# Row-shaped score matmuls with one late transpose, and four instead of five VectorE batches, in a decode attention kernel

## The chip, the cores and the metric

The kernel runs on one core of a Trainium2 chip. The metric is device time in microseconds (us): medians over several executions, with the lowest and highest beside them where they matter. Runs of one kernel are compared with runs of the kernel before on the same chip. Where a run is set against the changed kernel ("after"), the two were taken in different calls; the kernel before was timed in each of these calls, and its medians there lie between 2827.4 and 2829.4 us.

Engine names are those of the profile: PE is TensorE, DVE is VectorE, ACT is ScalarE, POOL is GpSimd, SP is the queue that issues the transfers.

## The reference

Two independent attention blocks, A and B, do one decode step each. For 8 batches and 32 heads, a query of 128 numbers meets 4096 cached keys and values. Everything is bf16.

```python
q = (x @ wq).reshape(B, Sq, H, Dh).transpose(0, 2, 1, 3)        # B=8, Sq=1, H=32, Dh=128
scores = jnp.einsum("bhqd,bhkd->bhqk", q, k_cache) * (Dh ** -0.5)   # Sk=4096 keys
p = softmax(scores, axis=-1)
o = jnp.einsum("bhqk,bhkd->bhqd", p, v_cache)
return o.transpose(0, 2, 1, 3).reshape(B, Sq, H * Dh) @ wo
# the outputs of A and B are concatenated
```

Each key and value is used once. K and V of one batch and head are 1 MB each; there are 2 x 32 x 8 = 512 such pairs, so 1,074 MB must be read whatever the arithmetic does.

## The kernel before

The kernel walks over 64 groups (one head of one block, 8 batches each), batch by batch. The scores of a batch are made on one of two paths. `DVB` lists the batches of each group that go to VectorE; the others go to TensorE.

The VectorE path makes one fused multiply-and-add instruction for each 128 keys. The profile shows two for it (L409 of the page below: 10,240 products and 10,240 reads of an accumulator in 320 VectorE batches), so a batch costs 64 instructions.

```python
NKB = 3
DVB = list(cfg.get("DVB", (1, 2, 4, 5, 7)))          # five of eight batches on VectorE
PEB = [b for b in range(NB) if b not in DVB]          # 0, 3, 6 on TensorE
# ... (cut)
def dqk_item(n, k):                                   # quarter k of VectorE batch n
    # ... (waits cut: K landed, q replicated, previous batch done)
    for jj in range(8):
        j = 8 * k + jj
        ins = d.tensor_tensor_reduce(junk[:, j, :], Kb[:, kslot, j * 128:(j + 1) * 128], q_rep[:, par, r, :],
                                     1.0, 0.0, ALU.mult, ALU.add, S2[:, par, r, j:j + 1])
```

The TensorE path transposes K (pairs of bf16 are moved as one f32), ScalarE copies the result from PSUM to SBUF (`KT`), and small matmuls make the scores, with K as the stationary operand and a query of two columns as the moving one.

```python
def emit_T(n, q):                                     # 4 transposes, q = 0..3
    # ... (cut)
    for tt in range(4):
        t = q * 4 + tt
        ins = pe.transpose(dst[:, tt * 128:(tt + 1) * 128], kf[:, t * 128:(t + 1) * 128], ident_f[:])
def emit_QK(n, q):                                    # 8 small matmuls
    # ... (cut)
    for tt in range(4):
        t = q * 4 + tt
        # ... (cut)
        for e in range(2):
            ins = pe.matmul(S[:, c:c + 2], lhsT=ktb[:, t * 256 + e:(t + 1) * 256:2],
                            rhs=Qe[:, G % 2, pe_rank[b], e, :], start=(e == 0), stop=(e == 1))
```

All transfers are issued by SP, in one order. K has 6 buffers (`NK`), V has 8. A buffer of K is free when its transposes (TensorE batch) or its dot products (VectorE batch) are done.

```python
w = [k_released(n - NK)] if n >= NK else []
# ... (cut)
sp.dma_start(Kb[:, n % NK, :], Ks[blk][b, h].rearrange("(p j) d -> p (j d)", p=128))
```

## Time and profile before

| | before |
|---|---|
| time, median of 15 runs | 2827.81 us (2822.08 to 2833.07) |
| VectorE busy, instructions | 80%, 20,935 |
| TensorE busy, instructions (matmuls and weight loads) | 68%, 2 x 15,328 |
| K and V transfers on q1, share of 16 DMA engines | 96.2% |
| instruction fetches: q8, q14 | 124, 204 packets |

These are lines of the profile's page. The first gives the span, the second the busy time of each engine with its share and instruction count. PEclk is the granted TensorE clock and DMA the busy share of the DMA engines, both in tenths for 40 equal slices of the span. The q lines are DMA queues: packets, MB, share of 16 engines. Then come the shares of the chain of waits, and groups of instructions (count, busy us, mean ns of one, idle time before them).

```profile
span 2829.2 us, 58099 instructions
PE 1921.2 (68%) x15328; PEld 1228.2 (43%) x15328; DVE 2271.6 (80%) x20935; ACT 685.6 (24%) x1997; POOL 52.1 (2%) x138
...
PEclk7888788887888887888778888888778887788888
DMA  9999999999999999998999989999899998999996
...
q1 hardware_dynamic: 165056, 1107.43, 96.2%
q8 instruction: 124, 2.03, 0.3%
q14 instruction: 204, 1.67, 0.1%
...
DMA 52%; DVE 31%; PE 13%; SPq 2%; issue 1%; ACT 0%; DVEq 0%; POOL 0%; POOLq 0%
...
L409 DVE CUSTOM_DVE_ANT_0 junk<-Kb,q_rep 128x128 bf16<-128x128 bf16 x10240 | 2211.2, 286 | 323.9 <-DMA Kb<-in_A_k_cache_dram 146.7
L269 PE MATMUL ps<-Vb,Ppad 128*32 128x512 bf16 x4096 | 1010.3, 397 | 7.1 <-ACT Ppad L385 3.0
L229 PE MATMUL ps<-ident_f,Kb 128*128 128x128 f32 x3072 | 621.5, 386 | 508.0 <-DMA Kb<-in_B_k_cache_dram 266.5
L409 DVE DVE_READ_ACCUMULATOR2_ANT S<- 128x1 f32 x10240 | 833.5, 81 | 0.1
...
L250 PE MATMUL ps<-Qe,KT 128*128 128x2 bf16 x6144 | 182.8, 163 | 0.2
```

No compute engine is full; the DMA engines nearly are. But "96% on average" hides something. The windows view shows the busy time of each engine in stretches of 10 us, and in its last three columns the granted clock, the DMA share and GB/s:

```profile
core 0: us, PE busy (x) PEld busy (x) DVE busy (x) ACT busy (x) POOL busy (x), PEclk, DMA share, GB/s
2020.00:2030.00 10.00, 3.70 (x22) 2.83 (x21) 9.94 (x95) 0.46 (x2) 0.00 (x0) 0.76 1.01 425
2030.00:2040.00 10.00, 8.71 (x76) 5.04 (x74) 7.18 (x68) 1.92 (x4) 0.00 (x0) 0.90 0.79 306
2040.00:2050.00 10.00, 5.75 (x27) 4.39 (x28) 8.86 (x84) 3.20 (x6) 0.00 (x0) 0.66 0.15 38
2050.00:2060.00 10.00, 3.38 (x44) 1.66 (x41) 6.85 (x63) 0.00 (x0) 0.37 (x1) 0.79 1.01 416
```

Between 2040 and 2050 us the DMA engines moved 38 GB/s instead of about 420. In 5-us windows the share goes down to 0.06 or 0.07, which is one engine of 16. Such a hole comes about every 350 us, some 15 us after SP issues each load of the next projection weights.

The landing records of the trace point to the engine whose part of a transfer lands last. They do not number the engines; that it is the same one each time is read from its even pace. The records hold 16 raises of a semaphore for each of the 1,096 transfers of K, V and the weights (17,536 of 17,572 records). I read each raise as one of the 16 engines whose own part has landed. That is a reading; what speaks for it is the spacing: in this run the fourteenth raise comes within about 2 us of the first (1.5 us on average), and the sixteenth on average 14.2 us after the fourteenth (and 13.8 us after the fifteenth). So read, one engine lags by some six 64-KB shares of a transfer. My reading of a hole is that the other fifteen have no work left that the buffers allow, and the last one catches up; inside it the trace's packets follow each other singly, 0.31 us per 8 KB.

The waits of the SP queue (who waited for whom: us, times, longest) say that the next K transfer is often held until VectorE frees a buffer. That can be read in two ways: VectorE is late, or the K data was late to VectorE because its sixteenth part was.

```profile
SPq L715 <- DVE S L409: 1269.4, 296, 22.7
SPq L720 <- PE ps L269: 305.8, 174, 9.9
...
SPq L715 <- PE ps L229: 21.1, 11, 9.2
```

### The profile page before, as it was taken

The numbers are of one execution on the slowest core, as the hardware profiler recorded it, in microseconds if no ns is written. First come the engines' busy times: TensorE is split into PE (matmuls) and PEld (weight loads), VectorE is DVE, ScalarE is ACT, GpSimd is POOL, SyncE is SP. The second block draws the span as 40 slices with busy tenths as digits, with TensorE's granted clock in tenths as the row PEclk, the third lists the DMA queues.
The fourth block names the chain that finished last, engine by engine and source line by source line (L and its number), as shares of the span: only waits on it lengthen the run. The fifth ranks groups of instructions, "written<-read, shape, count | busy, mean of one in ns | idle before, by whom it ended". The sixth has DMA issues, their size and how long they took to land.

```text
span 2829.2 us, 58099 instructions
## 1 busy us (share of the span) xinstructions
PE 1921.2 (68%) x15328; PEld 1228.2 (43%) x15328; DVE 2271.6 (80%) x20935; ACT 685.6 (24%) x1997; POOL 52.1 (2%) x138
## 2 busy tenths in 40 slices
PE   4676666766667676766767667776667667666666
PEld 3444444444344444444444444444444444444443
DVE  7988788877888878888787887888878888788885
ACT  2222222222122222222222222222222222222222
POOL 0000000000000000000000000000000000000000
PEclk7888788887888887888778888888778887788888
DMA  9999999999999999998999989999899998999996
GB/s 360 420 419 416 375 414 398 389 393 370 420 406 390 378 385 420 405 397 359 404 411 400 396 353 399 419 418 401 334 420 419 410 401 342 420 408 396 398 395 251
DMA packets 165384, 1111.13 MB, mean 393 GB/s; under 512 B 17568, under 2 KB 17568, under 8 KB 33984
## 3 DMA queue, kind: packets, MB, share of 16 engines
q1 hardware_dynamic: 165056, 1107.43, 96.2%
q8 instruction: 124, 2.03, 0.3%
q14 instruction: 204, 1.67, 0.1%
HBM read 1107.33 MB, written 0.03 MB: 391 GB/s over the span
## 4 chain that ended last, share of the span: by engine, by line
DMA 52%; DVE 31%; PE 13%; SPq 2%; issue 1%; ACT 0%; DVEq 0%; POOL 0%; POOLq 0%
DVE junk L409 30%; DMA Kb<-in_B_k_cache_dram 27%; DMA Kb<-in_A_k_cache_dram 24%; PE ps L229 7%; PE ps L269 5%; DVE S L409 1%; SPq L715 1%; SPq L720 1%; DMA Vb<-in_B_v_cache_dram 1%; PE ps L332 1%; DVE Qe L453 0%; DVE acc L476 0%; DVEq L755 0%; PE ps L312 0%; SPq L737 0%
## 5 line engine op out<-in xcount | busy, mean ns | idle before, releaser
L409 DVE CUSTOM_DVE_ANT_0 junk<-Kb,q_rep 128x128 bf16<-128x128 bf16 x10240 | 2211.2, 286 | 323.9 <-DMA Kb<-in_A_k_cache_dram 146.7
L269 PE MATMUL ps<-Vb,Ppad 128*32 128x512 bf16 x4096 | 1010.3, 397 | 7.1 <-ACT Ppad L385 3.0
L229 PE MATMUL ps<-ident_f,Kb 128*128 128x128 f32 x3072 | 621.5, 386 | 508.0 <-DMA Kb<-in_B_k_cache_dram 266.5
L409 DVE DVE_READ_ACCUMULATOR2_ANT S<- 128x1 f32 x10240 | 833.5, 81 | 0.1
L229 PEld LDWEIGHTS ps<-ident_f,Kb 128*128 128x128 f32 x3072 | 555.1, 205 | 548.6 <-DMA Kb<-in_B_k_cache_dram 284.7
L366 ACT COPY KT<-ps 128x512 f32<-128x512 f32 x768 | 436.5, 589 | 1192.9 <-PE ps L229 1192.7
L269 PEld LDWEIGHTS ps<-Vb,Ppad 128*32 128x32 bf16 x4096 | 379.9, 100 | 504.8 <-issue 138.2
L312 PE MATMUL ps<-ident,q_all 128*128 128x128 bf16 x320 | 54.2, 292 | 373.3 <-DVE Qe L453 324.2
L417 ACT CAST q_rep<-ps 128x512 bf16<-128x512 f32 (+1 forms) x128 | 54.6, 427 | 782.9 <-PE ps L312 782.9
L312 PEld LDWEIGHTS ps<-ident,q_all 128*128 128x128 bf16 x320 | 28.8, 122 | 392.5 <-DVE Qe L453 328.3
L250 PEld LDWEIGHTS ps<-Qe,KT 128*128 128x128 bf16 x6144 | 167.7, 97 | 54.2 <-issue 53.5
L250 PE MATMUL ps<-Qe,KT 128*128 128x2 bf16 x6144 | 182.8, 163 | 0.2
L476 DVE TENSOR_TENSOR acc<-ps,acc 128x64 f32<-128x64 f32 x62 | 13.9, 225 | 162.0 <-PE ps L332 162.0
L385 ACT ACTIVATE Ppad<-S,negM 128x32 bf16<-128x32 f32 x320 | 100.0, 318 | 0.0
L323 PEld LDWEIGHTS ps<-Sel,Dg_sb 32*128 32x128 f32 x512 | 61.6, 186 | 28.8 <-issue 26.5
L323 PE MATMUL ps<-Sel,Dg_sb 32*128 32x8 f32 x512 | 67.2, 253 | 4.0 <-ACT q_all L417 2.8
L695 POOL PARTITION_ALL_REDUCE M_sb<-m_sb x64 | 23.5, 367 | 2486.5 <-DVE m_sb L629 2486.5
L385 ACT ACTIVATION_READ_ACCUMULATOR Ppad<-S,negM 128x1 f32 x320 | 63.4, 198 | 0.0
L586 ACT COPY Dg_sb<-ps 32x512 f32<-32x512 f32 x64 | 36.8, 575 | 105.3 <-PE ps L269 105.3
L385 ACT ACTIVATE Ppad<-ps,negM 128x32 bf16<-128x32 f32 x192 | 54.6, 284 | 19.9 <-DVE negM L652 19.5
L385 ACT ACTIVATION_READ_ACCUMULATOR Ppad<-ps,negM 128x1 f32 x192 | 38.6, 201 | 0.0
L652 DVE TENSOR_SCALAR negM<-M_sb 128x8 f32<-128x8 f32 x64 | 11.0, 172 | 31.6 <-POOL M_sb L695 31.6
(36 smaller groups left out, 199.0 us busy)
## 6 DMA issues: line engine op xcount, KB each, us to landing
Kb<-in_A_k_cache_dram SPq DMA_DIRECT2D x256, 1024.0 KB, 24.8
Vb<-in_A_v_cache_dram SPq DMA_DIRECT2D x256, 1024.0 KB, 26.7
Kb<-in_B_k_cache_dram SPq DMA_DIRECT2D x256, 1024.0 KB, 25.1
Vb<-in_B_v_cache_dram SPq DMA_DIRECT2D x256, 1024.0 KB, 26.8
wq_sb<-in_A_wq_dram SPq DMA_DIRECT2D x4, 2048.0 KB, 32.4
wo_sb<-in_A_wo_dram SPq DMA_DIRECT2D x32, 256.0 KB, 25.3
wq_sb<-in_B_wq_dram SPq DMA_DIRECT2D x4, 2048.0 KB, 33.5
wo_sb<-in_B_wo_dram SPq DMA_DIRECT2D x32, 256.0 KB, 25.5
```

The source lines that it names most:

```text
L229: ins = pe.transpose(dst[:, tt * 128:(tt + 1) * 128], kf[:, t * 128:(t + 1) * 128], ident_f[:])
L250: ins = pe.matmul(S[:, c:c + 2], lhsT=ktb[:, t * 256 + e:(t + 1) * 256:2], rhs=Qe[:, G % 2, pe_rank[b], e, :], start=(e == 0), stop=(e == 1))
L269: ins = pe.matmul(Dg(par), lhsT=Ppad[:, par, b, c].rearrange("p a m -> p (a m)"), rhs=Vb[:, vslot, c * 512:(c + 1) * 512], start=(b == 0 a ...
L312: ins = pe.matmul(Mp_f[:, r * 128:(r + 1) * 128], lhsT=q_all[:, G, b:b + 1].broadcast_to([128, 128]), rhs=ident[:], start=True, stop=True)
L323: ins = pe.matmul(Mp_f[:, 0:NB], lhsT=Dg_sb[0:32, par, jj * 128:(jj + 1) * 128], rhs=Sel[0:32, jj, :], start=(jj == 0), stop=(jj == 3))
L332: ins = pe.matmul(Mp_f[:, c * NB:(c + 1) * NB], lhsT=wo_sb[:, G % 2, c * 128:(c + 1) * 128], rhs=oT[:, G % 2, :], start=True, stop=True)
L366: return a.copy(dst, src)
L385: return a.activation(Ppad[:, par, b, :, b, :], src.rearrange("p (c m) -> p c m", m=4), ACTF.Exp, bias=negM[:, par, pos[b]:pos[b] + 1], sc ...
L409: ins = d.tensor_tensor_reduce(junk[:, j, :], Kb[:, kslot, j * 128:(j + 1) * 128], q_rep[:, par, r, :], 1.0, 0.0, ALU.mult, ALU.add, S2[:, ...
L417: return eng.copy(dst, src) if COPY_ENG == "act" else eng.tensor_copy(dst, src)
L586: return a.copy(Dg_sb[:, G % 2, :], Dg(G % 2))
L715: return sp.dma_start(Kb[:, n % NK, :], Ks[blk][b, h].rearrange("(p j) d -> p (j d)", p=128))
```

## The change

The change has two parts. One batch of each group moves from VectorE to TensorE: VectorE keeps 1, 3, 5, 7. And the scores of a TensorE batch are made the other way round: the query is the stationary operand (32 columns, mostly zeros, one row for each batch and key position) and K the moving one, 512 columns at a time. All TensorE batches of a group accumulate into one PSUM bank, as rows; ScalarE copies the bank out and TensorE transposes it once per group. As that bank is taken from the K transposes, they have two banks instead of three. The intent is to relieve VectorE, the busiest compute engine, and to pay for it with fewer TensorE instructions.

```diff
-    NKB = 3
-    DVB = list(cfg.get("DVB", (1, 2, 4, 5, 7)))
+    NKB = 2
+    DVB = list(cfg.get("DVB", (1, 3, 5, 7)))
...
-                        t = q * 4 + tt
+                        t = 4 * tt + q
                         ins = pe.transpose(dst[:, tt * 128:(tt + 1) * 128], kf[:, t * 128:(t + 1) * 128], ident_f[:])
...
-                    for tt in range(4):
-                        t = q * 4 + tt
-                        c = b * NJ + 2 * t
-                        for e in range(2):
-                            ins = pe.matmul(S[:, c:c + 2], lhsT=ktb[:, t * 256 + e:(t + 1) * 256:2],
-                                            rhs=Qe[:, G % 2, pe_rank[b], e, :], start=(e == 0), stop=(e == 1))
+                    r = pe_rank[b]
+                    for e in range(2):
+                        first = (r == 0 and q == 0 and e == 0)
+                        last = (r == NPE - 1 and q == NQ - 1 and e == 1)
+                        ins = pe.matmul(Srow, lhsT=QeP[:, G % 2, r, e, q, :],
+                                        rhs=ktb[:, q * 1024 + e:(q + 1) * 1024:2],
+                                        start=first, stop=last, skip_group_check=True)
...
+        def emit_ST(G):
...
+                for tl in range(4):
+                    ins = pe.transpose(dst[:, tl * RW:(tl + 1) * RW], Srow_sb[0:RW, tl * 128:(tl + 1) * 128], ident_f[0:RW, 0:RW])
...
+                def f(a, G=G):
+                    return a.copy(Srow_sb[0:RW, :], Srow)
+                add("act", f"SREV{G}", w, [(act_sr, 1)], f)
```

Left out: the two query permutations (QP) become two bursts with a VectorE copy after each, the exponentials and the maximum read the transposed bank, and the waits follow.

More of the change, by code (lines that the diff above doesn't have):

```diff
@@ L100, in bass_concat_heads__mha_block_cached__mha_block_cached__decode_kernel @@
         HM2 = E(nc.sbuf_tensor("HM2", [128, 2], f32))
-        Qe = E(nc.sbuf_tensor("Qe", [128, 2, max(NPE, 1), 2, 2], bf16))
+        RW = 8 * max(NPE, 1)
+        QeP = E(nc.sbuf_tensor("QeP", [128, 2, max(NPE, 1), 2, 4, RW], bf16))
+        Srow_sb = E(nc.sbuf_tensor("Srow_sb", [32, 512], f32))
         acc = E(nc.sbuf_tensor("acc", [128, NBLK, NCO * NB], f32))
@@ L117, in Slin, with Sq @@
             return ps[:, 3 + par, :]
+        Srow = ps[0:RW, 2, :]
+        def Sq(par):
+            return ps[:, 3 + par, 0:4 * RW]
         def Dg(par):
@@ L140, in bass_concat_heads__mha_block_cached__mha_block_cached__decode_kernel @@
         s_hm = sem("s_hm")
+        act_sr, pe_st = sem("act_sr"), sem("pe_st")
         def head_info(n):
@@ L191, in bass_concat_heads__mha_block_cached__mha_block_cached__decode_kernel @@
             for G in range(NG):
-                pe_extras.setdefault(slot_QR(G), []).append(("QP", G))
+                for e in range(2):
+                    pe_extras.setdefault(slot_QR(G), []).append(("QP", (G, e)))
         for G in range(NG):
@@ L245, in f @@
                     ktb = KT[:, e_idx(n) % 2, :]
-                    for tt in range(4):
-                        t = q * 4 + tt
-                        c = b * NJ + 2 * t
-                        for e in range(2):
-                            ins = pe.matmul(S[:, c:c + 2], lhsT=ktb[:, t * 256 + e:(t + 1) * 256:2],
-                                            rhs=Qe[:, G % 2, pe_rank[b], e, :], start=(e == 0), stop=(e == 1))
+                    r = pe_rank[b]
+                    for e in range(2):
+                        first = (r == 0 and q == 0 and e == 0)
[3 more added lines that the diff above has]
+                                        start=first, stop=last, skip_group_check=True)
                     return ins
@@ L297, in emit_QS, with emit_QP, f @@
             return f
-        def emit_QP(G):
+        def emit_QP(G, e):
+            def f(pe):
+                return pe.matmul(Mp_f[:, 0:NB], lhsT=Perm[:, e, :], rhs=q_all[:, G, :], start=True, stop=True)
+            return f
+        def emit_ST(G):
+            par = G % 2
             def f(pe):
                 ins = None
-                for e in range(2):
-                    ins = pe.matmul(Mp_f[:, e * NB:(e + 1) * NB], lhsT=Perm[:, e, :], rhs=q_all[:, G, :],
-                                    start=True, stop=True)
+                dst = Sq(par)
+                for tl in range(4):
+                    ins = pe.transpose(dst[:, tl * RW:(tl + 1) * RW], Srow_sb[0:RW, tl * 128:(tl + 1) * 128], ident_f[0:RW, 0:RW])
                 return ins
@@ L378, in exp_item, with f @@
                     w.append((pool_L, G - 1))
-            if b in pe_rank:
-                src = Sp(par)[:, b, :]
-            else:
-                src = S2[:, par, dv_rank[b], :]
-            def f(a, G=G, b=b, par=par, src=src):
-                return a.activation(Ppad[:, par, b, :, b, :], src.rearrange("p (c m) -> p c m", m=4),
+            if b in pe_rank and T1:
+                src = Sq(par).rearrange("p (t h u r) -> p r t h u", t=4, h=2, u=4, r=NPE)[:, pe_rank[b]]
+                dst = Ppad[:, par, b, :, b, :].rearrange("p (t h) m -> p t h m", h=2)
+            elif b in pe_rank:
+                src = Sp(par)[:, b, :].rearrange("p (c m) -> p c m", m=4)
+                dst = Ppad[:, par, b, :, b, :]
+            else:
+                src = S2[:, par, dv_rank[b], :].rearrange("p (c m) -> p c m", m=4)
+                dst = Ppad[:, par, b, :, b, :]
+            def f(a, G=G, b=b, par=par, src=src, dst=dst):
+                return a.activation(dst, src,
                                     ACTF.Exp, bias=negM[:, par, pos[b]:pos[b] + 1], scale=SCALE,
@@ L444, in burst_reads, with f @@
                 elif kind == "QP":
-                    G = idx
-                    w = [rd_burst_wait(("QP", G))]
+                    G, e = idx
+                    w = [rd_burst_wait(("QP", (G, e)))]
                     if G >= 2:
                         w.append((pe_qk, NPE * (G - 1)))
-                    def f(d, G=G):
-                        src = Mp_f[:, 0:2 * NB].rearrange("p (e b) -> p b e", e=2)
-                        src = src[:, PEB[0]:PEB[0] + pe_step * (NPE - 1) + 1:pe_step, :]
-                        return d.tensor_tensor(Qe[:, G % 2], src.unsqueeze(3).broadcast_to([128, NPE, 2, 2]),
-                                               HM2[:, :].unsqueeze(1).unsqueeze(1).broadcast_to([128, NPE, 2, 2]), ALU.mult)
-                    add(which, f"QPC{G}", w, [(dve_mp, 1)], f)
+                    def f(d, G=G, e=e):
+                        src = Mp_f[:, PEB[0]:PEB[0] + pe_step * (NPE - 1) + 1:pe_step]
+                        dst = QeP[:, G % 2, :, e, :, :].rearrange("p r c (c2 j r2) -> p r c c2 j r2", r2=NPE, c2=4, j=2)
+                        base = dst[:, 0, 0, 0, :, 0]
+                        (ps_, pn_), (js_, jn_) = base.ap
+                        r_st = dst[:, :, 0, 0, 0, 0].ap[1][0] + dst[:, 0, 0, 0, 0, :].ap[1][0]
+                        c_st = dst[:, 0, :, 0, 0, 0].ap[1][0] + dst[:, 0, 0, :, 0, 0].ap[1][0]
+                        diag = bass.AP(base.tensor, base.offset, [[ps_, pn_], [r_st, NPE], [c_st, 4], [js_, jn_]])
+                        return d.tensor_tensor(diag, src.unsqueeze(2).unsqueeze(3).broadcast_to([128, NPE, 4, 2]),
+                                               HM2[:, :].unsqueeze(1).unsqueeze(1).broadcast_to([128, NPE, 4, 2]), ALU.mult)
+                    add(which, f"QPC{G}.{e}", w, [(dve_mp, 1)], f)
                 elif kind == "OEX":
@@ L517, in bass_concat_heads__mha_block_cached__mha_block_cached__decode_kernel @@
                     if q == 0:
-                        w.append(dve_done(("QP", G)) if T1 else dve_done(("QS", G // HQ)))
-                        if pe_rank[b] == 0 and G >= 2:
+                        w.append(dve_done(("QP", (G, 1))) if T1 else dve_done(("QS", G // HQ)))
+                        if pe_rank[b] == 0 and G >= 1 and T1:
+                            w.append((act_sr, G))
+                        if pe_rank[b] == 0 and G >= 2 and not T1:
                             w.append((sm_m, NSM * (G - 1)))
@@ L523, in bass_concat_heads__mha_block_cached__mha_block_cached__decode_kernel @@
                     add("pe", f"QK{n}.{q}", w, [(pe_qk, 1)] if q == NQ - 1 else [], emit_QK(n, q))
+                if T1 and pe_rank[b] == NPE - 1:
+                    w = [(act_sr, G + 1)]
+                    if G >= 2:
+                        w.append((sm_m, NSM * (G - 1)))
+                        w.append((act_P, NB * (G - 2) + NB))
+                    add("pe", f"ST{G}", w, [(pe_st, 1)], emit_ST(G))
             if DL <= i < N + DL:
@@ L540, in bass_concat_heads__mha_block_cached__mha_block_cached__decode_kernel @@
                 elif kind == "QP":
-                    G = idx
-                    w = [dve_done(("QS", G // HQ)), (s_hm, 1)] + pe_burst_waits(("QP", G))
-                    add("pe", f"QP{G}", w, [(pe_mp, 1)], emit_QP(G))
+                    G, e = idx
+                    w = [dve_done(("QS", G // HQ)), (s_hm, 1)] + pe_burst_waits(("QP", (G, e)))
+                    add("pe", f"QP{G}.{e}", w, [(pe_mp, 1)], emit_QP(G, e))
                 elif kind == "OEX":
@@ L577, in bass_concat_heads__mha_block_cached__mha_block_cached__decode_kernel @@
                     exp_item(Gx, b)
+            if T1 and NPE and 1 <= i <= N and is_pe(i - 1) and pe_rank[(i - 1) % NB] == NPE - 1:
+                G = (i - 1) // NB
+                w = [(pe_qk, NPE * (G + 1))]
+                if G >= 1:
+                    w.append((pe_st, G))
+                def f(a, G=G):
+                    return a.copy(Srow_sb[0:RW, :], Srow)
+                add("act", f"SREV{G}", w, [(act_sr, 1)], f)
             if COPY_ENG == "act":
@@ L595, in f @@
                 def f(d):
+                    return d.memset(QeP[:], 0.0)
+                add("dve", "init_qep", [], [(dve_init, 1)], f)
+                def f(d):
                     return d.memset(HM2[:], 0.0)
@@ L600, in f @@
                     return d.memset(HM2[0:64, 0:1], 1.0)
-                add("dve", "init_hm1", [(dve_init, 2)], [(dve_init, 1)], f)
+                add("dve", "init_hm1", [(dve_init, 3)], [(dve_init, 1)], f)
                 def f(d):
                     return d.memset(HM2[64:128, 1:2], 1.0)
-                add("dve", "init_hm2", [(dve_init, 2)], [(dve_init, 1)], f)
+                add("dve", "init_hm2", [(dve_init, 3)], [(dve_init, 1)], f)
                 def f(d):
                     return d.tensor_copy(ident_f[:], ident[:])
-                add("dve", "init_idf", [(s_id, 1), (dve_init, 4)], [(s_hm, 1)], f)
+                add("dve", "init_idf", [(s_id, 1), (dve_init, 5)], [(s_hm, 1)], f)
             dv_head = i < N and not is_pe(i)
@@ L614, in bass_concat_heads__mha_block_cached__mha_block_cached__decode_kernel @@
                 if NPE:
-                    w = [(pe_qk, NPE * (G + 1))]
+                    w = [(pe_st, G + 1)] if T1 else [(pe_qk, NPE * (G + 1))]
                     if G >= 2:
@@ L619, in f @@
                     def f(d, G=G, par=par):
+                        if T1:
+                            return d.tensor_reduce(m_sb[:, par, 0:NPE], Sq(par).rearrange("p (x r) -> p r x", r=NPE), AX.X, ALU.max)
                         return d.tensor_reduce(m_sb[:, par, 0:NPE],
```

## The prediction

> **What bounds it now.** The DMA engines do. The busy-share page has DVE at 80%, PE 68%, ACT 24%, but the DMA row is at 9 tenths or more nearly throughout and the queue table gives q1 96.2% of 16 engines. K and V alone are 1,074 MB; no arithmetic change removes a byte of them. The chain of waits agrees: 51% of it is K transfers, 30% the VectorE dot products, 12% PE.
>
> The packet records say more. Each transfer's semaphore is raised 16 times; 14 or 15 raises come within about 2 us, the last about 16 us later. One DMA engine lags. In the windows view it shows as holes (one near 2040 us, seven in all, about 350 us apart) where the DMA share falls to 0.06-0.07, one engine of 16, for about 10 us. Inside a hole the busy engine's packets follow each other at 306 ns per 8 KB, and one is an instruction fetch. Its lag grows about 2 us per 44-us group. Instruction fetches total 3.7 MB, at 306 ns per 8 KB an estimated 140 us for one engine. [...]this trace has 124 such packets on q8, and 8 KB ones on q14. So I read the pace as that one engine's: its sixteenth of the data plus the instruction fetches.
>
> **What the change does, per group of 8 batches.**
> - DVE: 5 dot-product heads become 4. One is 32 x 0.213 us = 6.8 us; busy should fall from 2272 to about 1840 us (65%). DVE is not the bound, so this frees little.
> - PE adds a fourth K transpose (16 per head, 3.4-3.6 us) and replaces 3 x 32 small matmuls (0.95 us per head) by 4 x 8 of 512 columns. PV, also 512 columns, takes 0.229 us each, so about 1.85 us per head. Adds the score transpose (estimate 0.5-1 us), a wait for its ACT copy (about 1 us), and a second QP/DVE round trip (about 0.5 us). It saves the 4.8 us that PE waited for the Qe copy, since batch 5 no longer follows another DVE batch. My sum of PE issue time and unavoidable waits is 41.5 us per group, against 44.1 us now observed. PE busy about 2400 us (85%), close to the bound but under it.
> - ACT: 768 to 1024 KT copies of 0.59 us, plus 64 copies; about 860 us. Two KT banks instead of three: copy and transposes are each about 0.6-0.85 us per quarter, estimated loss 0.1-0.3 us per head, on PE.
> - Instructions: PE about 30,700 to 25,000, DVE 20,900 to 16,900. At 64 bytes each, about 0.6 MB less to fetch by the lagging engine, worth about 24 us.
>
> **Critical path.** The DVE saving and the PE addition are both off it; only the fetch saving is on it. Prediction 2804 us, range 2778 to 2850. Faster by over 2%: 0.06; within 2%: 0.84; slower by over 2%: 0.10.
>
> **What would show it right.** DMA share still about 96%; holes still about 350 us apart; fewer instruction-queue packets (q8 about 102, q14 about 165); PE's waits for K and for Qe shrink; the sync queue's 1269 us of waits for DVE fall, while time hardly moves. Row matmuls near 0.23 us.
>
> **What would make it wrong.** Row matmuls read bf16 at stride 2; if that streams at half rate, PE gains 7 us per group and becomes the bound (over 3000 us). The same if bank waits or the two PE-DVE-ACT handshakes cost several us per group more. Faster, if the holes or the end tail come from late buffer release rather than from the lagging engine.

The sum is the 2828 us of the kernel before less the 24 us of fetches: 2804 us. The sizes it counts with are shown here: q8 moved 2.03 MB in 124 packets, so 16 KB each, q14 1.67 MB in 204, so 8 KB each (page before), and the 64 bytes of an instruction are measured in x_pe and few_before below.

## The result, and the profile after

| | before | after |
|---|---|---|
| time, median | 2827.81 us (15 runs) | 2788.69 us (8 runs, 2785.45 to 2794.04) |
| ratio, 95% interval | | 0.9864 (0.9854 to 0.9874) |
| VectorE busy, instructions | 80%, 20,935 | 67%, 16,904 |
| TensorE busy, instructions | 68%, 2 x 15,328 | 82%, 2 x 12,448 |
| q8, q14 packets | 124, 204 | 102, 176 |

Ratios are the mean time of one kernel's runs over that of the other's runs of the same rounds, so they are not quite the ratio of the medians quoted. The change gained 1.4%, 39 us between the medians. All outputs are right.

The same lines of the page of the changed kernel:

```profile
span 2784.4 us, 48947 instructions
PE 2276.8 (82%) x12448; PEld 1234.8 (44%) x12448; DVE 1861.2 (67%) x16904; ACT 826.2 (30%) x2253; POOL 51.7 (2%) x138
...
PEclk9999999998999989999999998999999999999999
DMA  9999999999999999998999989999899998999996
...
q1 hardware_dynamic: 165056, 1107.43, 96.8%
q8 instruction: 102, 1.67, 0.2%
q14 instruction: 176, 1.44, 0.1%
...
DMA 63%; PE 20%; DVE 12%; SPq 2%; ACT 1%; issue 1%; POOL 0%; DVEq 0%; ACTq 0%; POOLq 0%
...
L431 DVE CUSTOM_DVE_ANT_0 junk<-Kb,q_rep 128x128 bf16<-128x128 bf16 x8192 | 1770.2, 286 | 345.6 <-DMA Kb<-in_B_k_cache_dram 167.3
L279 PE MATMUL ps<-Vb,Ppad 128*32 128x512 bf16 x4096 | 1024.6, 396 | 1.1 <-issue 0.7
L238 PE MATMUL ps<-ident_f,Kb 128*128 128x128 f32 x4096 | 674.8, 320 | 387.3 <-DMA Kb<-in_B_k_cache_dram 173.0
...
L259 PE MATMUL ps<-KT,QeP 128*32 128x512 bf16 x2048 | 507.7, 389 | 0.0
```

VectorE lost 410 us of busy time and TensorE gained 356 us, and the time followed neither. The DMA row is digit for digit the same, and so are the holes. Here is one in the windows view of the changed kernel, with the same columns:

```profile
1650.00:1660.00 10.00, 8.08 (x46) 4.32 (x47) 7.28 (x66) 2.25 (x4) 0.00 (x0) 0.88 1.01 398
1660.00:1670.00 10.00, 8.89 (x49) 4.58 (x48) 6.02 (x55) 2.64 (x5) 0.00 (x0) 0.95 0.09 38
1670.00:1680.00 10.00, 4.96 (x25) 1.97 (x22) 8.74 (x80) 0.57 (x1) 0.36 (x1) 0.91 0.92 355
```

The SP queue's waits for VectorE fell by 284 us, seven times the gain. More than half of that moved to TensorE, whose transposes now free more of the K buffers (21.1 us before, 172.6 after), so the waits for K buffers fell by about 133 us in all:

```profile
SPq L765 <- DVE S L431: 985.2, 232, 10.9
SPq L770 <- PE ps L279: 263.3, 159, 7.1
SPq L765 <- PE ps L238: 172.6, 52, 20.8
```

**Where the 39 us come from.** Take the sixteenth landing of every transfer of the trace, put them in order of time, and look at the steps from one to the next. I read that as the progress of the lagging engine. A 1024-KB transfer gives it 64 KB, and most steps are 2.48 us long. Apart from the smaller and larger transfers of the weights, the exceptions are nearly all of one kind (the counts are worked out from the landing records and the DMA packet records of the two traces):

```
steps between sixteenth landings      before             after
2.4 to 2.6 us                         832, mean 2.483    883, mean 2.483
2.6 to 3.2 us                         26                 8
3.2 to 4.0 us                         163, mean 3.465    132, mean 3.455
   of these with a q14 fetch in them  161                129
sum of all steps, us                  2818.1             2773.3
```

The sum of the steps is by construction the time from the first of these landings to the last; that most have one of two lengths, and only 9 before and 8 after are over 4 us, says, on this reading, that this engine is hardly ever idle. A long step costs 0.98 us more than an ordinary one (3.465 - 2.483), and nearly each (161 of 163) holds the end of a q14 packet, that is an instruction fetch of 8 KB (q14 on the page: kind instruction, 1.67 MB in 204 packets). Before, 163 long steps cost 160 us in excess; after, 132 cost 128 us. These 32 us are most of the 44.8 us by which the two profiled executions differ. VectorE's code of 20,935 instructions at 64 bytes each is 164 blocks of 8 KB, and of 16,904 it is 132. (The 64 bytes are measured below: on VectorE in few_before, with 140 packets of 8 KB less for 17,920 instructions less, and on TensorE in x_pe.) The long steps count VectorE's code.

The packet records show one such step from inside. In a hole the DMA share is that of one engine (0.07 from 1690 to 1695 us), and its packets stand alone. In the hole near 1696 us of the kernel before, data packets of 8 KB take 0.31 us each; then comes a q14 packet of 0.33 us, and the data packet after it takes 0.97 us instead of 0.31. Together that is the 0.98 us of a long step. Six q14 packets stand alone in this trace: the next data packet takes 0.97 us after five of them and 0.87 us after the one in the hole near 2040 us; why it takes longer stays open.

That is an observation of two traces. The experiments had to show that it is the cause, and that it is VectorE's instruction count and not its work.

### The profile page after: what moved, and what is told of

Same layout as the page of the kernel before. It is cut to its first block, busy times and chain, and to the rows that moved or that the text cites. A ratio compares the mean times of both kernels' runs of the same rounds, so it can differ in the third digit from the quotient of the medians.

```text
span 2784.4 us, 48947 instructions
## 1 busy us (share of the span) xinstructions
PE 2276.8 (82%) x12448; PEld 1234.8 (44%) x12448; DVE 1861.2 (67%) x16904; ACT 826.2 (30%) x2253; POOL 51.7 (2%) x138
## 3 DMA queue, kind: packets, MB, share of 16 engines
q8 instruction: 102, 1.67, 0.2%
## 4 chain that ended last, share of the span: by engine, by line
DMA 63%; PE 20%; DVE 12%; SPq 2%; ACT 1%; issue 1%; POOL 0%; DVEq 0%; ACTq 0%; POOLq 0%
DMA Kb<-in_B_k_cache_dram 33%; DMA Kb<-in_A_k_cache_dram 30%; DVE junk L431 11%; PE ps L279 8%; PE ps L238 6%; PE ps L259 3%; SPq L770 2%; PE ps L340 1%; ACT KT L383 1%; SPq L765 1%; DMA Vb<-in_B_v_cache_dram 1%; DVE S L431 1%; PE ps L302 0%; PE ps L349 0%; DVE acc L503 0%
## 5 line engine op out<-in xcount | busy, mean ns | idle before, releaser
L431 DVE CUSTOM_DVE_ANT_0 junk<-Kb,q_rep 128x128 bf16<-128x128 bf16 x8192 | 1770.2, 286 | 345.6 <-DMA Kb<-in_B_k_cache_dram 167.3
L238 PE MATMUL ps<-ident_f,Kb 128*128 128x128 f32 x4096 | 674.8, 320 | 387.3 <-DMA Kb<-in_B_k_cache_dram 173.0
L383 ACT COPY KT<-ps 128x512 f32<-128x512 f32 x1024 | 564.7, 587 | 1127.9 <-PE ps L238 1126.2
L238 PEld LDWEIGHTS ps<-ident_f,Kb 128*128 128x128 f32 x4096 | 523.2, 161 | 539.8 <-DMA Kb<-in_B_k_cache_dram 208.7
L431 DVE DVE_READ_ACCUMULATOR2_ANT S<- 128x1 f32 x8192 | 666.7, 81 | 0.1
L259 PE MATMUL ps<-KT,QeP 128*32 128x512 bf16 x2048 | 507.7, 389 | 0.0
L259 PEld LDWEIGHTS ps<-KT,QeP 128*32 128x32 bf16 x2048 | 189.4, 95 | 249.9 <-issue 4.3
L439 ACT CAST q_rep<-ps 128x512 bf16<-128x512 f32 x64 | 37.4, 585 | 400.3 <-PE ps L329 400.3
L620 ACT COPY Srow_sb<-ps 32x512 f32<-32x512 f32 x64 | 36.7, 574 | 205.1 <-PE ps L259 205.1
L480 DVE TENSOR_TENSOR QeP<-ps,HM 128x32 bf16<-128x32 f32 x128 | 29.3, 229 | 84.7 <-PE ps L311 84.7
```

What stands on the lines that cost most here:

```text
L259: ins = pe.matmul(Srow, lhsT=QeP[:, G % 2, r, e, q, :], rhs=ktb[:, q * 1024 + e:(q + 1) * 1024:2], start=first, stop=last, skip_group_chec ...
L383: return a.copy(dst, src)
L439: return eng.copy(dst, src) if COPY_ENG == "act" else eng.tensor_copy(dst, src)
L620: return a.copy(Srow_sb[0:RW, :], Srow)
```

## The experiments

Theory V: one of the 16 DMA engines carries VectorE's instruction fetches besides its sixteenth of the data; each 8-KB block costs it about 1 us, and it paces the kernel. Rival F is the prediction's own version: all engines' code weighs on that engine, at the rate of data. Rival R: the row matmuls bring the gain. Rival B: VectorE's busy time decides, through the late release of K buffers. A further rival, that VectorE itself stalls for its next instructions, does not show in the traces: its idle time in which it waited for nothing that the profile shows ("issue") is 0.5 us in the kernel before and 3.1 us in x_tiny below. Ten kernels were run, all with three timed rounds; all gave correct results.

### Each half of the change alone: x_dve4 and x_row5

x_dve4 is the kernel before with four VectorE batches, still with small score matmuls and three banks:

```diff
-    DVB = list(cfg.get("DVB", (1, 2, 4, 5, 7)))
+    DVB = list(cfg.get("DVB", (1, 3, 5, 7)))
```

> The kernel before with one edit: batches 1,3,5,7 instead of 1,2,4,5,7 go to VectorE; scores of the TensorE batches stay small column matmuls, three KT banks. TensorE gets about 36,800 instructions (30,700 before, 24,900 after), VectorE about 16,850 (20,900 before). Theory V (the pace is set by the one DMA engine that also carries VectorE's instruction fetches, about 0.97 us per 8 KB block): about 132 blocks instead of 164, 31 us or a little more saved, 2787 to 2797 us, as after. Rival F (my prediction: all fetches weigh on that engine by their bytes): 0.39 MB more for TensorE, 0.26 MB less for VectorE, no gain, 2825 to 2835 us. Rival R (the row matmuls themselves bring the gain): 2825 us.

Measured: 2785.21 us, ratio to before 0.9854 (0.9837 to 0.9871), q8 148 and q14 174 packets, 2 us below V's range. One line of the kernel before gives the whole gain.

x_row5 is the changed kernel with the five VectorE batches put back:

```diff
-    DVB = list(cfg.get("DVB", (1, 3, 5, 7)))
+    DVB = list(cfg.get("DVB", (1, 2, 4, 5, 7)))
```

> The changed kernel with one edit back: batches 1,2,4,5,7 on VectorE, so row matmuls and transposed scores but five VectorE batches. VectorE about 21,000 instructions, TensorE about 20,000. Theory V: 164 or 165 blocks as before, so 2818 to 2832 us, no gain over before. Rival F: 0.65 MB less TensorE code than before at 306 ns per 8 KB is 24 us less, about 2802 us. Rival R: about 2790 us.

Measured: 2828.12 us, ratio 1.0003 (0.9988 to 1.0018), q8 90 and q14 206. The row matmuls and the late transpose are worth nothing in time here. Rivals F and R both fall with this pair: TensorE's fetches went from 124 to 148 in one kernel and to 90 in the other, and the time moved with q14 alone. What is left between V and B is whether VectorE's instructions or its work count.

### Instructions without work, work without instructions: x_tiny and x_long

x_tiny adds 16 one-element memsets to each VectorE batch of the changed kernel:

```diff
                 ins = None
+                for zz in range(4):
+                    d.memset(scr[:, 4 * k + zz:4 * k + zz + 1], 0.0)
                 for jj in range(8):
```

> The changed kernel with 4096 one-element memsets (16 in each VectorE head) on VectorE[...]: back to about 21,000 VectorE instructions and 164 blocks, VectorE busy up by about 250 us to about 2110 us, below the 2272 us of before. Theory V: 31 us slower than after, 2815 to 2825 us. Rival F: 0.26 MB at 306 ns per 8 KB, 10 us slower, about 2799 us. Rival B (VectorE's busy time decides, through late release of K buffers): between after and before, slower by 15 to 30 us; told apart by x_long.

Measured: 2823.59 us, 34.9 us slower than after; ratio to before 0.9986 (0.9972 to 1.0001). The memsets took almost no time of their own on VectorE, less than I had expected: busy time is 1902.7 us, only 41 us above the changed kernel (10 ns for each of the 4,096) and 369 us below the kernel before, and yet the time is back at about the old value. These lines are of its page:

```profile
PE 2293.5 (81%) x12448; PEld 1244.8 (44%) x12448; DVE 1902.7 (67%) x21000; ACT 831.9 (29%) x2253; POOL 52.4 (2%) x138
...
q14 instruction: 208, 1.70, 0.2%
```

x_long adds the work with few instructions, two memsets of 640 f32 elements for each VectorE batch:

```diff
+            if k % 2 == 1:
+                add("dve", f"LONG{n}.{k}", [(dve_z, n_long[0])] if n_long[0] else [], [(dve_z, 1)],
+                    lambda d: d.memset(scr[:], 0.0))
+                n_long[0] += 1
```

> The changed kernel with 512 memsets of 640 f32 elements (2 in each VectorE head), about 0.5 us each: about the same added VectorE time as x_tiny (about 280 us) in 512 instructions, 4 blocks. Theory V: 4 us slower than after, 2789 to 2796 us. Rival B: as slow as x_tiny, 2805 to 2820 us.

Measured: 2800.42 us, 11.7 us slower than after, with VectorE busy 2132.7 us (76%) and 180 q14 packets:

```profile
PE 2274.1 (81%) x12448; PEld 1234.8 (44%) x12448; DVE 2132.7 (76%) x17416; ACT 829.0 (30%) x2253; POOL 58.7 (2%) x138
...
q14 instruction: 180, 1.47, 0.1%
```

So 271 us more of work (0.53 us for each of the 512 memsets) cost 11.7 us, of which 4 would be due to the four more fetches; 41 us more of work in 4,096 instructions cost 34.9 us. V's forecast for x_long (up to 2796) was missed by 4 us, so work on VectorE is not quite free. But rival B, as the main cause, is out: x_tiny is much slower than x_long with less busy time.

### Nearly no VectorE instructions: few_after, few_before, few_dve4

The dot products are written as 4 multiplies and 4 reductions per batch, which is 8 instructions instead of 64. The three kernels have the same edit, in the changed kernel, in the kernel before, and in x_dve4.

```diff
-                for jj in range(8):
-                    j = 8 * k + jj
-                    ins = d.tensor_tensor_reduce(junk[:, j, :], Kb[:, kslot, j * 128:(j + 1) * 128], q_rep[:, par, r, :],
-                                                 1.0, 0.0, ALU.mult, ALU.add, S2[:, par, r, j:j + 1])
+                return d.tensor_tensor(junk[:, 8 * k:8 * k + 8, :],
+                                       Kb[:, kslot, k * 1024:(k + 1) * 1024].rearrange("p (j d) -> p j d", d=128),
+                                       q_rep[:, par, r, :].unsqueeze(1).broadcast_to([128, 8, 128]), ALU.mult)
+            # one quarter later, after a wait on the multiply:
+                    return d.tensor_reduce(S2[:, par, r, 8 * kk:8 * kk + 8], junk[:, 8 * kk:8 * kk + 8, :], AX.X, ALU.add)
```

> The changed kernel with the VectorE dot products written as 4 multiplies (128x1024 bf16) and 4 reductions per head instead of 32 fused instructions with 32 accumulator reads: about 2,600 VectorE instructions instead of 16,900, 20 blocks of code instead of 132, VectorE busy about as before (estimate 1700 to 2000 us). Products are rounded to bf16 before the sum, so the result may differ slightly. Theory V (0.97 us of the pacing DMA engine per VectorE block): 112 blocks less are 109 us less, 2675 to 2690 us. If TensorE's 102 fetches (16 KB, about 1 us each) all sit on one other engine, that engine paces next and the time stops at 2720 to 2760 us. Rival B (VectorE's busy time decides): no change beyond what busy time changes, 2780 to 2800 us.

> The same rewriting in the kernel before, five VectorE batches: about 3,100 instructions, 24 blocks instead of 164. Theory V: 136 us less, 2690 to 2705 us, so it beats the changed kernel without any of the change; with VectorE busier (estimate 2100 to 2300 us). Rival B: 2800 to 2830 us.

> x_dve4 (four VectorE batches, small score matmuls) with the same rewriting: 20 VectorE blocks, TensorE about 36,800 instructions (148 fetches against 102 in few_after). Theory V: as few_after within 0.5%. If TensorE's fetches pace next: slower than few_after by 25 to 45 us.

Measured: few_after 2672.44 us, ratio 0.9449 (0.9435 to 0.9463). few_before 2680.72 us, ratio 0.9478 (0.9464 to 0.9492). few_dve4 2679.50 us, ratio 0.9469 (0.9453 to 0.9485). The first two were a little faster than V's forecast, and the third is within 0.5% of few_after as it should be. The forecast had used 0.97 us for a block, and here it is 1.05 ((2827.8 - 2680.7) / (204 - 64) for few_before). few_before does more work on VectorE than the kernel before (2306 against 2272 us busy, 86% of its span) and is 147 us faster: the strongest single piece of evidence against rival B. From its page:

```profile
PE 1888.5 (70%) x15328; PEld 1201.7 (45%) x15328; DVE 2306.1 (86%) x3015; ACT 681.1 (25%) x1997; POOL 61.2 (2%) x138
...
q14 instruction: 64, 0.52, 0.0%
```

The page of few_after, where the GB/s row gives the rate in each of the 40 slices:

```profile
span 2669.5 us, 34611 instructions
PE 2215.7 (83%) x12448; PEld 1194.6 (45%) x12448; DVE 1887.9 (71%) x2568; ACT 825.4 (31%) x2253; POOL 62.6 (2%) x138
...
DMA  9999999999999999999999999999999999999997
GB/s 383 420 420 420 417 421 420 420 420 417 421 420 420 419 416 420 421 420 416 415 421 420 420 412 418 420 421 420 413 420 420 421 420 410 421 420 420 421 420 321
...
q1 hardware_dynamic: 165056, 1107.43, 100.3%
q8 instruction: 102, 1.67, 0.3%
q14 instruction: 64, 0.52, 0.0%
```

The holes are gone, the rate is at 420 GB/s in nearly every slice, and the sixteenth landing comes on average 2.6 us after the fourteenth instead of 14.2 us. There are 25 long steps left. At 420 GB/s the 1,107 MB alone take 2637 us, so this kernel is within about 35 us of that; at that rate there is little left to gain without reading less.

few_dve4 fetches 46 more TensorE blocks than few_after and is 7 us slower (0.3%). I had named 25 to 45 us as the sign that TensorE's fetches pace next; they do not. (The "about 1 us" for a fetch of 16 KB is as measured: 1.03 us in the kernel before and 1.07 us in the changed one, medians of the q8 packets.)

### Six batches on TensorE: pe6

```diff
-    DVB = list(cfg.get("DVB", (1, 2, 4, 5, 7)))
+    DVB = list(cfg.get("DVB", (6, 7)))
```

> The kernel before with only batches 6 and 7 on VectorE, six on TensorE with small score matmuls: VectorE about 8,750 instructions, 68 blocks. Theory V: 95 blocks less are 92 us less, 2730 to 2745 us, unless TensorE (six transposed heads of 2.3 to 3.5 us, 0.95 us of score matmuls each, 14.7 us of value matmuls and about 3 us of the rest, 37 to 44 us per group) becomes the bound: then up to 2850 us. VectorE busy falls to about 1000 us; Rival B would give at most what TensorE allows, so this run only tests the count against the time.

Measured: 2723.30 us, ratio 0.9628 (0.9614 to 0.9643), with VectorE at 8,647 instructions and 36% busy, TensorE at 83%, and q8 at 196, q14 at 117 packets. The time is 7 us below V's range. The step from after is 65.4 us; VectorE's 8,257 instructions less are 64.5 blocks, so 1.01 us each. (q14 fell by only 59 packets; it also carries code of ScalarE, which has 448 instructions more.) TensorE carried it, so my upper figure for TensorE (44 us per group) did not hold.

### Code of the other engines: x_pe and x_act

x_pe adds 12 two-column matmuls ahead of each batch's value matmuls, into an unused part of the bank:

```diff
+                for zz in range(12):
+                    pe.matmul(ps[32:64, 5 + par, 2 * zz:2 * zz + 2], lhsT=ident[:, 0:32], rhs=ident[:, 0:2],
+                              start=True, stop=True, skip_group_check=True)
```

> The changed kernel with 12 two-column matmuls (12 weight loads) ahead of each head's value matmuls, into an unused quadrant: 12,288 more TensorE instructions, 48 more fetches of 16 KB on q8, TensorE busy up by an estimated 150 to 190 us. Theory V (only VectorE's code rides on the pacing DMA engine): same as after within 0.3%, 2782 to 2797 us. Rival F (all code weighs on it by bytes, 0.79 MB more at 306 ns per 8 KB): 29 us slower, about 2818 us.

Measured: 2788.28 us, the same as after (2788.69). Its queue lines:

```profile
q8 instruction: 150, 2.46, 0.4%
q14 instruction: 176, 1.44, 0.1%
```

The 12,288 added instructions brought 48 packets of 16 KB, so 64 bytes each, and all on q8. Its long steps are 132 in number, exactly as many as after. The 6,144 tiny matmuls took 32 us of TensorE's busy time, less than the 150 to 190 that I had expected (in the kernel before, as many two-column matmuls are busy for 182.8 us, L250).

x_act adds 2048 one-element copies to ScalarE, four ahead of each exponential:

```diff
+                for zz in range(4):
+                    a.copy(scr[:, par, b, zz:zz + 1], negM[:, par, 0:1])
```

> The changed kernel with 2048 one-element copies on ScalarE, 4 ahead of each exponential ([...]410 us more busy, 30% to about 45%): 16 more blocks of 8 KB on q14. If ScalarE's code rides on the same engine as VectorE's: 16 us slower than after, 2802 to 2808 us. If it rides elsewhere: 2786 to 2794 us. In the packet records: q14 up to 192 in both cases.

Measured: 2791.61 us, ratio to before 0.9876 (0.9857 to 0.9896), which overlaps the interval of after. The copies took 182 us of ScalarE's busy time (0.09 us each), not the 410 that I had expected. q14 rose to 192 packets as expected, but the long steps did not (again 132). So q14 carries the code of VectorE and of ScalarE, and only VectorE's blocks delay the engine that paces this kernel.

### All kernels side by side

| kernel | us | VectorE instructions | VectorE busy, us | q8 | q14 | long steps |
|---|---|---|---|---|---|---|
| before | 2827.8 | 20,935 | 2272 | 124 | 204 | 163 |
| x_row5 | 2828.1 | 21,000 | 2288 | 90 | 206 | 162 |
| x_tiny | 2823.6 | 21,000 | 1903 | 103 | 208 | 167 |
| x_long | 2800.4 | 17,416 | 2133 | 102 | 180 | 135 |
| x_act | 2791.6 | 16,904 | 1862 | 102 | 192 | 132 |
| after | 2788.7 | 16,904 | 1861 | 102 | 176 | 132 |
| x_pe | 2788.3 | 16,904 | 1862 | 150 | 176 | 132 |
| x_dve4 | 2785.2 | 16,839 | 1841 | 148 | 174 | 131 |
| pe6 | 2723.3 | 8,647 | 971 | 196 | 117 | 65 |
| few_before | 2680.7 | 3,015 | 2306 | 124 | 64 | 27 |
| few_dve4 | 2679.5 | 2,503 | 1867 | 148 | 62 | 11 |
| few_after | 2672.4 | 2,568 | 1888 | 102 | 64 | 25 |

The time follows the third column, to within 9 us of a straight line through before and few_before, and neither the busy time nor q8. The last column counts the steps of 3.2 to 4.0 us, worked out from every trace as above. Down to pe6 it is VectorE's instructions over 128, to within 3; in the three few_ kernels the last landing lags by only 2 to 4 us, and the count is looser.

## Why the prediction was right or wrong

The forecast time, 2804 us with a range of 2778 to 2850, held the measured 2788.69 us, and "within 2%" was right. Point by point:

- **The bound.** "The DMA engines do", and in particular one lagging engine with "its sixteenth of the data plus the instruction fetches": right. Busy times moved by hundreds of microseconds in both directions without the time following.
- **The step that was mis-sized** is "about 0.6 MB less to fetch by the lagging engine, worth about 24 us". It was wrong in two ways that partly cancelled. It charged TensorE's code to that engine, 14 of the 24 us (5,760 instructions less, 45 times 8 KB at 306 ns); x_pe (48 more blocks, no change) shows that this costs nothing. And it charged 306 ns for 8 KB, the spacing of data packets, so only 10 us for VectorE's code; the longer data packet after each fetch was missing. A VectorE block cost 0.98 us in the steps of the trace and 1.09 us in x_tiny (34.9 us for 32 blocks). VectorE's 32 blocks at 1.09 us are 35 of the 39 us. That the sum of 24 us came so near the 39 measured was in part luck. Had TensorE's code shrunk and VectorE's not, as in x_row5, the same step would have promised about 21 us (8,704 instructions of 64 bytes less on TensorE, at 306 ns per 8 KB) and given none.
- **The rest of the gain**, about 4 us, is the difference between x_row5 (2828.1) and x_tiny (2823.6), which have the same 21,000 instructions but five and four VectorE batches. Steps of 2.6 to 3.2 us are 26 in before and in x_row5, with five batches, and 6 to 8 in x_tiny and after. That neighbouring VectorE batches free their buffers late is a likely reason; it was argued, not shown.
- **TensorE** was forecast at about 2400 us busy; it was 2277. The row matmuls were right: eight take about 1.8 us from their start to the next instruction, as the value matmuls do (on the page 389 ns busy each, against 396), so a moving operand at stride 2 cost nothing here. The transposes were not: I took 3.4 to 3.6 us for 16 from the kernel before. There 16 transposes took a median of 3.65 us in the 106 batches in which the trace's clock record grants 0.5 throughout, and of 1.99 us in the 46 in which it grants 1.0. The mean granted clock was 0.81 before and is 0.92 after; what sets it was not shown. The timeline (start and duration in us) has 16 transposes in 3.65 us before, where the clock record grants 0.5, and 8 in 1.07 us after, where it grants 1.0. First the line before, then the lines after:

```profile
2000.82 3.65 PE L229 MATMUL ps<-ident_f,Kb 128*128 128x128 f32 x16
```

```profile
1053.26 1.07 PE L238 MATMUL ps<-ident_f,Kb 128*128 128x128 f32 x8
1054.57 1.14 PE L238 MATMUL ps<-ident_f,Kb 128*128 128x128 f32 x8 [0.24 <-ACT KT L383]
1055.64 1.90 PE L279 MATMUL ps<-Vb,Ppad 128*32 128x512 bf16 x8
1057.38 1.96 PE L259 MATMUL ps<-KT,QeP 128*32 128x512 bf16 x8
```

- The bracket on the second line is a wait that two banks bring instead of three: 0.24 us for ScalarE's copy. Over the trace TensorE waited 51.4 us for these copies, 0.20 us per TensorE batch, in the forecast range of 0.1 to 0.3. But from first to last, 16 transposes at a granted clock of 1.0 took 2.48 us instead of 1.99 (medians), 0.40 us of it between the start of the eighth and of the ninth. So the price was about 0.5 us per batch, above the forecast. It cost the kernel little: ScalarE is 1% of the chain that ended last.
- **VectorE** at about 1840 us (1861), **ScalarE** at about 860 us (826), q8 at 102 (102) and q14 at about 165 (176), holes at the same spacing, the SP queue's waits for VectorE down, TensorE's waits for K (508 to 335 us) and for the Qe copy (324 to 57 us) down: as predicted. That SP's waits for K buffers fell by 133 us while the time fell by 39 speaks against these waits as the cause; that the data they waited to replace had itself come late is my reading of it.

## What to carry to other kernels

When a kernel is bound by transfers, compare the landing of the last part of each transfer with that of the others: here an average share of 96.2% was, as I read the landings, one engine that was hardly ever idle and fifteen that waited for it. The instructions of this long unrolled program were data too: 328 packets, 3.7 MB, on q8 and q14 in the kernel before. Each 128 VectorE instructions cost about 1 us (0.98 to 1.09 in the runs above), dot products and one-element memsets alike, and replacing 64 small ones by 8 large ones gave nearly four times the gain of the change in the kernel before (147 us against 39), and a further 116 us in the changed kernel.
